# A fused attention and mixture kernel on one Trainium2 core: keys and queries loaded in whole rows, heads multiplied in 64-row tiles

## The chip, the cores and the metric

The kernel runs on one core of a Trainium2 chip. The metric is the device time of one execution in microseconds, and the time of a kernel is the median of its runs. TensorE (PE) multiplies; VectorE (DVE), ScalarE (ACT) and GpSimd (POOL) do the elementwise work; SyncE (SP) and POOL issue the transfers.

## The reference, cut to what matters

Two attentions with 32 packed queries per head, then a feed-forward layer, then a mixture of eight experts. Only the attention and what it hands on are touched by the change.

```python
def sm_attn(qq, kk, vv):                      # softmax(qq kk^T / sqrt(64)) vv
    ...
p_packed = sm_attn(p, k, v)                   # p: 4 x 8 x 32 x 64, k and v: 4 x 8 x 576 x 64
out = sm_attn(q, p_packed, p_packed)          # q: 4 x 8 x 576 x 64
x = out.transpose(0, 2, 1, 3).reshape(2304, 512)
h = x @ moe_w_in                              # 512 x 2048, in 64-bit floats
x = (h * clip(h + 3, 0, 6) / 6) @ moe_w_out   # 2048 x 512
...                                           # routing and eight experts, 512 x 1024 x 512 each
```

## The kernel before, in words

**An order written by a planner.** The kernel is a list of operations with costs, priorities, buffers and dependences. `Order.run` walks through it when the kernel is built, with a clock for each engine (PE, DVE, ACT, POOL, and SP for its transfers), and takes at each step the operation that can start first. The result is a fixed order of instructions on each engine. On the chip an engine doesn't skip an instruction that still waits, so what stands behind it waits too. `copy` (lines 439 to 447) lets the planner put an eviction on ACT or DVE. `dma` (line 436) gives each transfer on SP a cost from the KiB named to it.

**Attention in eight units.** `attention(u)` (from line 639) does unit u = 2b + j, four heads of batch b. Its keys lie as `kp[g]`: 96 partitions of 6 positions each, and for each position the two heads of a pair side by side. The queries lie as `qp`: two halves of 64 partitions with 9 positions each, also with the heads of a pair side by side. Each head is loaded by its own DMA on SP (lines 657 to 664 and 687 to 695), whose contiguous pieces on the SBUF side are one position of one head, 64 floats or 256 bytes. Values (line 698) come in one DMA with six positions of a head, 1536 bytes, in a piece. Unit 1 uses buffers that are free early; units 0 and 2 to 7 share one set of k, q and v buffers.

**The steps of a unit on PE.** Keys are transposed (L721) and evicted to `kT`, with the 2 x 64 features of a pair on the partitions. The packed queries, doubled side by side by a POOL copy (L706), are transposed (L738), and multiplied by `maskb` while they are evicted (L743), so that a matmul over 128 rows picks one head of the pair. First scores are four matmuls, 128 rows by 64 columns (L763). Then come maximum, exponential and sum (L773 to L801); query transposes (L811) and their evictions to `qT`; transposes of the exponentials (L831); products with the values (L847), each for both heads of a pair, so that half of the result belongs to the wrong head; scaling by the reciprocal and by `maskz`, which zeroes that half (L858); two transposes (L872) and two evictions to `ppT`; second scores over 128 rows (L904); and a second softmax whose result is the operand `a2` of the first layer.

**Packed weights.** `packed_weights` (line 994) multiplies the packed values with the first-layer weights. For the first units of work it is called with one weight block, takes one PSUM bank and does four matmuls of 128 rows by 64 columns (L1008). Later it is called with two blocks, takes two banks, and does 64-row by 32-column tiles (L1014). The results are evicted by ACT (L1031) and DVE (L1036). Layers 1 and 2 (L1074 to L1076, L1108 to L1110, L1127 to L1129) follow.

**Around it.** While attention runs, 64-bit weights are loaded in pieces of 512 KB. Sixteen of these are issued by POOL (L533) and taken apart by ACT (L506, L510), DVE (L513, L514, L517) and POOL (L501). Attention's units, this decoding and the first layers stand mixed in each engine's order.

Of the kernel before, what the change touches and what calls it, by code (L numbers as in the profile page):

```python
# [67 lines left out]
V_KIB = 840  # L68
# [103 lines left out]
def tile_kernel(  # L172
# [168 lines left out]
    maskb = [x.tile([128, 2, NP], F32, name=f"maskb{i}") for i, x in enumerate((const, att))]  # L341
    maskz = [x.tile([128, 2, 2, D], F32, name=f"maskz{i}") for i, x in enumerate((const, att))]
# [294 lines left out]
    ppTs = [hold("ppT", [128, 2, 64]) for _ in range(NU)]  # L637

    def attention(u, p_sb):
# [13 lines left out]
        kp = [tile_of(f"k{g}", [PR, R, 2, D]) for g in range(2)]  # L653
        v_sb = tile_of("v", [PR, 4, R, D])
        qp = tile_of("q", [128, RQ, 2, D])
        pd = tile_of("pd", [128, 2, D], 2)
        for h in range(4):
            dma(
                288,
                lambda h=h: nc.sync.dma_start(  # L660
                    kp[h // 2].t[:, :, h % 2, :], k[b, 4 * j + h].rearrange("(p r) d -> p r d", r=R)
                ),
                fills=[kp[h // 2]], **kw,
            )
# [22 lines left out]
        for h in range(4):  # L687
            dma(
                288,
                lambda h=h: nc.sync.dma_start(  # L690
                    qp.t[64 * (h // 2):64 * (h // 2) + 64, :, h % 2, :],
                    q[b, 4 * j + h].rearrange("(p r) d -> p r d", r=RQ),
                ),
                fills=[qp], **kw,
            )
# [18 lines left out]
        kT = tile_of("kT", [128, 2, S])  # L714
        for g in range(2):
            for a in range(2):
                ps = bank()

                def trans(g=g, a=a, ps=ps):
                    for r in range(3):  # L720
                        nc.tensor.transpose(  # L721
                            ps.t[:, r * PR:(r + 1) * PR],
                            kp[g].t[:, 3 * a + r].rearrange("p h d -> p (h d)"),
                            ident[:PR, :PR],
                        )

                pe(0.25, trans, reads=[kp[g]], writes=[ps], takes=[kT], **kw)
                copy(
                    lambda g=g, a=a: kT.t[:, g, a * HS:(a + 1) * HS],
                    lambda ps=ps: ps.t[:, :HS], HS, reads=[ps], fills=[kT], **kw,  # L730
                )


        ps = bank()
        pt = tile_of("pt", [128, 2, 2 * NP], 2)
# [5 lines left out]
        dve(  # L741
            t_dve(128),
            lambda ps=ps: nc.vector.tensor_tensor(  # L743
                pt.t,
                ps.t[:, :128].rearrange("p (g c) -> p g c", g=2),
                maskb[j].rearrange("p h n -> p (h n)")[:, None, :].to_broadcast([128, 2, 2 * NP]),
                ALU.mult,
            ),
            reads=[ps], writes=[pt], **kw,
        )  # L750

# [7 lines left out]
        for a in range(2):  # L759

            def scores(a=a):
                for g in range(2):
                    nc.tensor.matmul(  # L763
                        s1[a].t[64 * g:64 * g + 64, :HS],
                        pt.t[:, g, :],
                        kT.t[:, g, a * HS:(a + 1) * HS],
                        start=True, stop=True,
                    )
# [35 lines left out]
        qT = tile_of("qT", [128, 2, S])  # L804
        for r0 in range(0, RQ, 4):
            n = min(4, RQ - r0)
            ps = bank()

            def trans(r0=r0, n=n, ps=ps):
                for r in range(n):  # L810
                    nc.tensor.transpose(  # L811
                        ps.t[:, r * 128:(r + 1) * 128],
                        qp.t[:, r0 + r].rearrange("p h d -> p (h d)"),
                        ident,
                    )

            pe(0.11 * n, trans, reads=[qp], writes=[ps], takes=[qT], **kw)
            copy(
                lambda r0=r0, n=n: qT.t.rearrange("p g (r c) -> p g r c", c=64)[:, :, r0:r0 + n, :],
                lambda n=n, ps=ps: ps.t[:, :n * 128].rearrange("p (r g c) -> p g r c", g=2, c=64),  # L820
                n * 128, reads=[ps], fills=[qT], **kw,
            )
# [21 lines left out]
        def packed():  # L844
            for r in range(R):
                for g in range(2):
                    nc.tensor.matmul(  # L847
                        pp.t[64 * g:64 * g + 64, :128],
                        a1T.t[:, r, 64 * g:64 * g + 64],
                        v_sb.t[:, 2 * g:2 * g + 2, r, :],  # L850
                        start=(r == 0), stop=(r == R - 1),
                    )

        ppz = tile_of("ppz", [128, 2, 2 * D], 2)
        pe(1.55, packed, reads=[a1T, v_sb], writes=[pp], takes=[ppz], **kw)
        dve(
            t_dve(256),
            lambda: nc.vector.scalar_tensor_tensor(  # L858
                ppz.t,
                pp.t[:, None, :128].to_broadcast([128, 2, 128]),  # L860
                rc.t,
                maskz[j].rearrange("p g h d -> p g (h d)"),
                ALU.mult, ALU.mult,
            ),
# [4 lines left out]

        def trans(ps=ps):  # L870
            for g in range(2):
                nc.tensor.transpose(ps.t[:, 128 * g:128 * g + 128], ppz.t[:, g, :], ident)  # L872

        pe(0.22, trans, reads=[ppz], writes=[ps], takes=[ppT], **kw)

        for g in range(2):
            copy(
                lambda g=g: ppT.t[:, g, :],
                lambda g=g, ps=ps: ps.t[:, 128 * g + 64 * g:128 * g + 64 * g + 64],
                64, reads=[ps], fills=[ppT], **kw,  # L880
            )
# [4 lines left out]
        for tiles in (range(0, 6), range(6, RQ)):  # L886
# [10 lines left out]
            def scores(s2=s2, pairs=pairs, tail=tail):  # L897
                todo = [
                    (w, 128 * i + 64 * g, t + w, g) for i, t in enumerate(pairs) for g in range(2) for w in range(2)
                ]  # L900
                if tail:
                    todo += [(g, 128 * len(pairs), RQ - 1, g) for g in range(2)]
                for w, c, t, g in todo:
                    nc.tensor.matmul(  # L904
                        s2.t[64 * w:64 * w + 64, c:c + 64],
                        qT.t[:, g, 64 * t:64 * t + 64],
                        ppT.t[:, g, :],
                        start=True, stop=True,
                    )
# [84 lines left out]
    def packed_weights(i, b, w1s):  # L994
# [4 lines left out]
        tiled = len(w1s) > 1  # L999
        banks, got = [psum("ph") for _ in range(2 if tiled else 1)], [pair("pw", [128, 2, FG]) for _ in w1s]  # L1000

        def mm():
            for x, w1 in enumerate(w1s):
                for g in range(2):
                    for j in range(2):
                        pp = ppTs[2 * b + j].t[:, g, :]
                        if not tiled:
                            nc.tensor.matmul(  # L1008
                                banks[0].t[64 * g:64 * g + 64, j * FG:(j + 1) * FG], pp, w1.t[:, 2 * j + g, :],
                                start=True, stop=True,  # L1010
                            )
                        for h in range(2 * tiled):
                            r0, n0 = 64 * h, 32 * (h ^ j)
                            nc.tensor.matmul(  # L1014
                                banks[j].t[64 * g + n0:64 * g + n0 + 32, x * FG:(x + 1) * FG],
                                pp[r0:r0 + 64, n0:n0 + 32],
# [23 lines left out]
        for x, w in enumerate(got):  # L1040
            if not tiled:
                out_of(
                    banks[0], lambda: banks[0].t,
                    lambda i, w=w: w.t[i].rearrange("p j f -> p (j f)"), 2 * FG,
                )
            for j in range(2 * tiled):
# [721 lines left out]
    with tc.manual_schedule():  # L1768
# [3 lines left out]
        for j in range(2):  # L1772
            nc.vector.memset(maskb[j], 0.0)
            for h in range(2):
                nc.vector.memset(maskb[j][64 * h:64 * h + 64, h ^ j, :], 1.0)
            nc.vector.memset(maskz[j], 0.0)
            for g in range(2):
                for h in range(2):
                    r0 = 64 * g + 32 * h
                    nc.vector.memset(maskz[j][r0:r0 + 32, g, h ^ j, :], 1.0)  # L1780

# [201 lines left out]
```

## Time and profile before

| | us |
|---|---|
| median of 3 runs | 1895.11 |
| lowest and highest | 1893.11, 1896.27 |
| the profiled execution's own time | 1896.55 |
| its span, first to last instruction | 1894.8 |
| PE busy | 1860.7 (98%) |
| DVE, ACT, POOL busy | 1452.2, 884.4, 1202.6 |

The times are for all three layers; attention ends within the first 140 us. A share of busy time is an average over stages with different limits, so the first 107 us are read below in stretches of their own. In the rows, PE is the matmuls and PEld the weight loads, and a number in brackets with an arrow is the time that an engine sat idle before the instruction, and what ended it.

### The profile page before, as it was taken

The page shows a single profiled execution, that of the slowest core. Times are in us where ns is not written, and L with a number is a line of the kernel's source. Part 1 is how long each engine was busy: PE and PEld are TensorE (multiplying, and loading weights), DVE is VectorE, ACT ScalarE, POOL GpSimd, SP SyncE. Part 2 cuts the span into 40 slices and gives each one's busy share as a digit, 9 for nine tenths or more (in the row PEclk, how much of TensorE's full clock was granted, in tenths as well). Part 3 has the DMA queues.
Part 4 walks back from the last instruction along what each step waited for, and adds up shares of the span by engine and source line. Part 5 has one row for each costly group of instructions (what it writes and reads, how often), then busy time and mean ns, then how long its engine had stood idle before and what let it go on. Part 6 is the DMA issues. An engine that isn't in the chain of part 4 may idle for free.

```text
span 1894.8 us, 31056 instructions
## 1 busy us (share of the span) xinstructions
PE 1860.7 (98%) x11199; PEld 1772.8 (94%) x11199; DVE 1452.2 (77%) x2367; ACT 884.4 (47%) x1931; POOL 1202.6 (63%) x1101
## 2 busy tenths in 40 slices
PE   6999999999999999999999999999999999999998
PEld 4889999898989999999999999999999999999998
DVE  5877687666887777787777877878797787787877
ACT  5765664455556565556543333333334233333332
POOL 3536586665768786778664665656676566565664
PEclk9999999999999999999999999999999999999999
DMA  9844335633677777877787777777778777777773
GB/s 207 204 117 145 128 105 206 223 129 134 210 248 283 269 273 247 300 271 262 276 306 249 264 257 268 252 257 261 263 246 276 252 258 264 261 256 258 261 252 109
DMA packets 190874, 440.70 MB, mean 233 GB/s; under 512 B 51728, under 2 KB 98976, under 8 KB 178432
## 3 DMA queue, kind: packets, MB, share of 16 engines
q1 hardware_dynamic: 187760, 429.31, 67.4%
q0 software_dynamic: 2480, 8.62, 1.6%
q8 instruction: 88, 1.44, 0.3%
q10 hardware_dynamic: 480, 0.79, 0.1%
q14 instruction: 66, 0.54, 0.1%
HBM read 316.42 MB, written 122.23 MB: 232 GB/s over the span
## 4 chain that ended last, share of the span: by engine, by line
PE 86%; DVE 4%; DMA 3%; POOL 3%; ACT 2%; issue 1%; SPq 1%; DVEq 0%; POOLq 0%; ACTq 0%
PE ph L1261 12%; PE ph L1259 12%; PE ph L1260 12%; PE po L1505 8%; PE po L1506 8%; PE po L1504 8%; PE po L1612 5%; PE po L1614 5%; PE po L1613 5%; PE po L1127 1%; PE po L1128 1%; PE po L1129 1%; DMA rawE<-in_moe_w_dram 1%; PE ph L1074 1%; PE ph L1076 1%
## 5 line engine op out<-in xcount | busy, mean ns | idle before, releaser
L1459 POOL TENSOR_TENSOR tmp<-tmp,tmp 128x384 f32<-128x384 f32 x153 | 168.7, 1103 | 354.5 <-DVE tmp L1236 353.4
L579 POOL TENSOR_TENSOR hs<-tmp,hs 128x384 fp32r<-128x384 f32 x212 | 232.6, 1100 | 170.8 <-ACT hs L574 163.9
L1446 ACT ACTIVATE xy<-tmp 128x384 fp32r<-128x384 f32 x324 | 162.1, 521 | 323.8 <-DVE tmp L1236 285.6
L1453 POOL TENSOR_TENSOR xy<-tmp,xy 128x384 fp32r<-128x384 f32 x228 | 275.4, 1220 | 7.3 <-ACT xy L1446 5.0
L1516 DVE TENSOR_TENSOR acc<-po,acc 128x384 f32<-128x384 f32 x302 | 165.8, 550 | 99.3 <-PE po L1506 97.9
L1273 DVE TENSOR_TENSOR tmp<-ph,tmp 128x384 f32<-128x384 f32 x288 | 159.5, 554 | 86.2 <-PE ph L1261 84.6
L453 ACT ACTIVATE tmp<-ph 128x384 f32<-128x384 f32 x280 | 137.1, 490 | 172.7 <-PE ph L1261 169.0
L1504 PE MATMUL po<-xy,w2s 128*128 128x384 f32 x640 | 215.0, 336 | 1.3 <-ACT tmp L453 1.3
L1506 PE MATMUL po<-xy,w2s 128*128 128x384 f32 x640 | 215.6, 337 | 0.0
L1505 PE MATMUL po<-xy,w2s 128*128 128x384 f32 x640 | 215.5, 337 | 0.0
L1261 PE MATMUL ph<-ax,w 128*128 128x384 f32 x576 | 193.5, 336 | 0.0
L1259 PE MATMUL ph<-ax,w 128*128 128x384 f32 x576 | 193.4, 336 | 0.0
L1260 PE MATMUL ph<-ax,w 128*128 128x384 f32 x576 | 193.2, 335 | 0.0
L1636 DVE SCALAR_TENSOR_TENSOR acc<-po,Pr,acc 128x512 f32<-128x512 f32 x168 | 125.0, 745 | 73.8 <-PE po L1614 73.6
L1612 PE MATMUL po<-w,hs 128*128 128x512 f32 x384 | 151.4, 394 | 0.0
L1614 PE MATMUL po<-w,hs 128*128 128x512 f32 x384 | 150.8, 393 | 0.0
L1613 PE MATMUL po<-w,hs 128*128 128x512 f32 x384 | 149.9, 390 | 0.0
L1236 DVE SCALAR_TENSOR_TENSOR tmp<-tmp,PB 128x384 f32<-128x384 f32 x192 | 138.6, 722 | 5.3
L574 ACT ACTIVATE hs<-tmp 128x384 fp32r<-128x384 f32 x224 | 117.1, 524 | 51.0 <-DVE tmp L1088 46.2
L1446 ACT ACTIVATE ax<-tmp 128x384 fp32r<-128x384 f32 x124 | 62.8, 521 | 142.0 <-DVE tmp L1236 129.9
L1504 PEld LDWEIGHTS po<-xy,w2s 128*128 128x128 f32 x640 | 120.2, 188 | 1.7 <-ACT tmp L453 1.6
L1505 PEld LDWEIGHTS po<-xy,w2s 128*128 128x128 f32 x640 | 120.3, 188 | 0.0
(276 smaller groups left out, 5445.2 us busy)
## 6 DMA issues: line engine op xcount, KB each, us to landing
w2s<-w2d SPq DMA_DIRECT2D x224, 512.0 KB, 4.5
w<-w1d SPq DMA_DIRECT2D x64, 1024.0 KB, 6.0
w1x<-w1d SPq DMA_DIRECT2D x64, 768.0 KB, 5.7
raw<-in_moe_w_dram SPq DMA_DIRECT2D x64, 512.0 KB, 6.5
w1d<-w SPq DMA_DIRECT2D x32, 1024.0 KB, 5.0
w2d<-w SPq DMA_DIRECT2D x96, 256.0 KB, 2.5
w1d<-w1x SPq DMA_DIRECT2D x32, 768.0 KB, 5.6
rawE<-in_moe_w_dram SPq DMA_DIRECT2D x20, 512.0 KB, 4.6
```

Source lines behind the costliest of these rows:

```text
L579: lambda e: e.tensor_tensor(dst(w.t[1]), src(), as_f32(dst(w.t[0])), ALU.subtract),
L1259: nc.tensor.matmul(out, wh[:, at + c, :], bh[:, c, :], start=first and c == 0, **on)
L1260: nc.tensor.matmul(out, wh[:, at + c, :], bl[:, c, :], start=False, **on)
L1261: nc.tensor.matmul(out, wl[:, at + c, :], bh[:, c, :], start=False, **on)
L1446: A_SBUF, lambda: nc.scalar.activation(dst(0), t.t, AF.Copy),
L1453: lambda e: e.tensor_tensor(dst(1), t.t, as_f32(dst(0)), ALU.subtract),
L1504: nc.tensor.matmul(o, wh[:, f, cs], ah[:, f, :], start=begin and f == 0, **on)
L1505: nc.tensor.matmul(o, wh[:, f, cs], al[:, f, :], start=False, **on)
L1506: nc.tensor.matmul(o, wl[:, f, cs], ah[:, f, :], start=False, **on)
L1612: nc.tensor.matmul(ps.t, hh[:, f, ts], wh[:, f, :], start=(f == 0), stop=False)
L1613: nc.tensor.matmul(ps.t, hh[:, f, ts], wl[:, f, :], start=False, stop=False)
L1614: nc.tensor.matmul(ps.t, hl[:, f, ts], wh[:, f, :], start=False, stop=(f == NFC - 1))
```

## The change

Keys and queries are loaded two heads at a time, each partition taking its 6 or 9 positions of a head as one contiguous piece (1536 and 2304 bytes). On the partitions after the transpose stand two positions of one head, in place of one position of two heads. So a matmul works on 64 rows: the packed queries and values stand twice, once for each half, and no mask is needed. The masks and their memsets go, and a tile `spare` of 64 floats takes some of their room. Each part of the diff, cut to its core:

```diff
-        for h in range(4):
-            dma(288, lambda h=h: nc.sync.dma_start(
-                kp[h // 2].t[:, :, h % 2, :], k[b, 4 * j + h].rearrange("(p r) d -> p r d", r=R)), ...
+        for g in range(2):
+            dma(V_KIB / 2, lambda g=g: nc.sync.dma_start(
+                kp[g].t.rearrange("p h r d -> p h (r d)"),
+                k[b, 4 * j + 2 * g:4 * j + 2 * g + 2].rearrange("h (p r) d -> p h (r d)", r=R)), ...
@@ queries alike: two DMAs in place of four @@
-        dve(t_dve(128), lambda: tensor_tensor(pt.t, ps..., maskb[j]..., ALU.mult), ...)
+        copy(lambda: pt.t..., lambda ps=ps: ps.t[:, :128], 128, ...)
 first scores, for each of two banks a
-                for g in range(2):
-                    nc.tensor.matmul(s1[a].t[64 * g:64 * g + 64, :HS],
-                        pt.t[:, g, :], kT.t[:, g, a * HS:(a + 1) * HS], ...)
+                rows = slice(64 * a, 64 * a + 64)
+                for x in range(4):
+                    nc.tensor.matmul(s1[a].t[32 * x:32 * x + 32, :HS],
+                        pt.t[rows, x, :], kT.t[rows, x ^ j, :], ...)
 queries: 8 transposes of 128 x 128 as before and, for the ninth position, in place of one more:
+            for g in range(2):
+                for hh in range(2):
+                    nc.tensor.transpose(ps.t[:64 * g + 64, ...], qp.t[:, hh, RQ - 1 - g:]..., ident)
+        for g in range(2):
+            copy(lambda half=half: qT.t[half, RQ - 1]..., ..., 128, ...)
 products with the values, for each of six r
-                for g in range(2):
-                    nc.tensor.matmul(pp.t[64 * g:64 * g + 64, :128],
-                        a1T.t[:, r, 64 * g:64 * g + 64], v_sb.t[:, 2 * g:2 * g + 2, r, :], ...)
+                for x in range(4):
+                    nc.tensor.matmul(pp.t[32 * x:32 * x + 32, :D],
+                        a1T.t[:, r, 32 * x:32 * x + 32], v_sb.t[:, x ^ j, 2 * (r % 3) + r // 3, :], ...)
-        dve(t_dve(256), lambda: scalar_tensor_tensor(ppz.t, pp..., rc.t, maskz[j]..., ...))
+        dve(t_dve(128), lambda: tensor_scalar_mul(ppz.t, pp.t[:, None, :D].to_broadcast([128, 2, D]), rc.t), ...)
 ppT: one transpose and one copy of 128 x 128 in place of two transposes and two copies of 128 x 64
 second scores: 36 matmuls of 64 rows and 32 columns of ppT in place of 18 of 128 rows and 64 columns
-                        s2.t[64 * w:64 * w + 64, c:c + 64], qT.t[:, g, 64 * t:64 * t + 64], ppT.t[:, g, :],
+                        s2.t[r0:r0 + 64, c:c + 32], qT.t[r0:r0 + 64, r, at:at + 64], ppT.t[r0:r0 + 64, x, :],
@@ packed_weights: always the tiled form @@
-        banks, got = [psum("ph") for _ in range(2 if tiled else 1)], ...
+        banks, got = [psum("ph") for _ in range(2)], ...
+                                banks[j].t[32 * n0:32 * n0 + 32, x * FG:(x + 1) * FG],
+                                ppTs[2 * b + j].t[r0:r0 + 64, n0, :], w1.t[r0:r0 + 64, 2 * j + g, :], ...
```

V_KIB is 840. In second scores r0 is 0 or 64, for the rows and for the output's partitions alike. A call of `packed_weights` with one weight block does eight tiled matmuls in place of four, and evicts two results of 256 columns in place of one of 512.

## Rows read from the trace of the kernel before

**Rows 1.** The page's 40 slices of the span, 47.4 us each, in tenths busy.
```profile
PE   6999999999999999999999999999999999999998
DMA  9844335633677777877787777777778777777773
```
**Rows 2.** Busy time by stretch; columns: us, PE, PEld, DVE, ACT, POOL, PEclk, DMA share, GB/s.
```profile
30.00:40.00 10.00, 9.24 (x91) 7.08 (x91) 9.22 (x18) 6.03 (x15) 6.86 (x6) 0.66 1.14 199
100.00:107.00 7.00, 4.67 (x20) 4.45 (x21) 7.00 (x21) 5.12 (x13) 3.93 (x5) 0.77 0.30 94
0.00:52.00 52.00, 34.78 (x296) 25.01 (x297) 29.80 (x96) 28.33 (x70) 19.04 (x31) 0.91 1.09 203
52.00:107.00 55.00, 52.05 (x512) 44.43 (x512) 47.89 (x125) 42.38 (x110) 28.85 (x32) 0.97 0.83 195
```
**Rows 3.** Timeline of PE: start, us, line, and the idle time before it.
```profile
18.48 0.69 PE L721 MATMUL tp<-ident,unit_hs 96*128 96x96 f32 x6 [1.13 <-DMA unit_hs<-in_k_dram]
20.39 0.44 PE L721 MATMUL tp<-ident,unit_hs 96*128 96x96 f32 x3 [1.22 <-DMA unit_hs<-in_k_dram]
43.74 0.69 PE L721 MATMUL tp<-ident,k 96*128 96x96 f32 x6 [2.02 <-DMA k<-in_k_dram]
47.49 0.69 PE L721 MATMUL tp<-ident,k 96*128 96x96 f32 x6 [1.65 <-DMA k<-in_k_dram]
101.44 1.06 PE L811 MATMUL tp<-ident,q 128*128 128x128 f32 x8 [1.63 <-issue]
103.39 0.44 PE L1074 MATMUL ph<-ax,pwh 128*128 128x384 f32 x1 [0.89 <-DVE tmp L1088]
```
**Rows 4.** Timeline of the first 8 us: transfers on SP, and POOL's first copy.
```profile
0.74 2.75 SPq L660 DMA_DIRECT2D k<-in_k_dram  x4
...
7.73 0.28 POOL L706 COPY pd<-p 128x128 f32<-128x128 f32 x1 [2.93 <-DMA p<-in_p_dram]
```
**Rows 5.** DMA view of 20 to 33 us: packets, queues (packets, MB, share of 16 engines), keys' issues.
```profile
DMA packets 5735, 2.92 MB, mean 225 GB/s; under 512 B 5093, under 2 KB 5477, under 8 KB 5733
...
q1 hardware_dynamic: 5445, 1.85, 90.1%
q0 software_dynamic: 288, 1.05, 28.5%
...
k<-in_k_dram SPq DMA_DIRECT2D x4, 144.0 KB, 9.3
```
**Rows 6.** Two links of the chain that ended last, in order of time: start, us, what.
```profile
35.82 11.53 DMA k<-in_k_dram
...
90.02 8.48 DMA raw<-in_moe_w_in_dram
```
**Rows 7.** Timeline of PE: one call each of the products that the change touches.
```profile
67.21 1.14 PE L811 MATMUL tp<-ident,q 128*128 128x128 f32 x9
68.61 1.09 PE L1008 MATMUL ph<-w1f,ppT 128*64 128x256 f32 x8
72.22 1.53 PE L847 MATMUL tp<-v,a1T 96*64 96x128 f32 x24
77.08 1.27 PE L904 MATMUL tp<-ppT,qT 128*64 128x64 f32 x36
78.17 1.14 PE L763 MATMUL tp<-kT,pt 128*64 128x288 f32 x8
165.35 1.09 PE L1014 MATMUL ph<-w1f,ppT 64*32 64x256 f32 x32
```
**Rows 8.** Groups by line and shape, 0 to 135 us: count, busy us and mean ns, idle before.
```profile
L743 DVE TENSOR_TENSOR pt<-tp,maskb 128x128 f32<-128x128 f32 x8 | 2.3, 292 | 6.2 <-PE tp L738 6.2
L858 DVE SCALAR_TENSOR_TENSOR ppz<-tp,rc,maskz 128x256 f32<-128x256 f32 x8 | 3.8, 478 | 1.8 <-PE tp L847 1.8
L443 ACT ACTIVATE qT<-tp 128x128 f32<-128x128 f32 x6 | 1.7, 276 | 0.9 <-PE tp L811 0.9
L1031 ACT ACTIVATE pwh<-ph 128x512 fp32r<-128x512 f32 x6 | 3.6, 606 | 0.2 <-PE ph L1008 0.2
```

More of the change, by code (lines that the diff above doesn't have):

```diff
@@ L340, in tile_kernel @@
     ones = const.tile([128, 128], F32, name="ones")
-    maskb = [x.tile([128, 2, NP], F32, name=f"maskb{i}") for i, x in enumerate((const, att))]
-    maskz = [x.tile([128, 2, 2, D], F32, name=f"maskz{i}") for i, x in enumerate((const, att))]
+    const.tile([128, 64], F32, name="spare")
     biases = const.tile([128, 2], F32, name="biases")
@@ L635, in operand @@
         return pair("xy", [128, KC // 2, TB])
-    ppTs = [hold("ppT", [128, 2, 64]) for _ in range(NU)]
+    ppTs = [hold("ppT", [128, 4, NP]) for _ in range(NU)]
     def attention(u, p_sb):
@@ L686, in attention @@
         p_at = b if j else max(b - 1, 0)
-        for h in range(4):
+        for g in range(2):
             dma(
[L689 to L692, printed above, removed]
+                V_KIB / 2,
+                lambda g=g: nc.sync.dma_start(
+                    qp.t[64 * g:64 * g + 64].rearrange("p h r d -> p h (r d)"),
+                    q[b, 4 * j + 2 * g:4 * j + 2 * g + 2].rearrange("h (p r) d -> p h (r d)", r=RQ),
                 ),
@@ L711, in attention, with trans @@
         turns.setdefault("pd0", turns["pd"])
-        kT = tile_of("kT", [128, 2, S])
-        for g in range(2):
[L716 to L731, printed above, removed]
+        kT = tile_of("kT", [128, 4, HS])
+        for h in range(4):
+            ps = bank()
+            def trans(h=h, ps=ps):
+                for r in range(R // 2):
+                    nc.tensor.transpose(
+                        ps.t[:, r * PR:(r + 1) * PR],
+                        kp[h // 2].t[:, h % 2, 2 * r:2 * r + 2].rearrange("p r d -> p (r d)"),
+                        ident[:PR, :PR],
+                    )
+            pe(0.25, trans, reads=[kp[h // 2]], writes=[ps], takes=[kT], **kw)
+            copy(lambda h=h: kT.t[:, h], lambda ps=ps: ps.t[:, :HS], HS, reads=[ps], fills=[kT], **kw)
         ps = bank()
-        pt = tile_of("pt", [128, 2, 2 * NP], 2)
+        pt = tile_of("pt", [128, 4, NP], 2)
         pe(
@@ L740, in attention @@
         )
[L741 to L749, printed above, removed]
+        copy(
+            lambda: pt.t.rearrange("p x n -> p (x n)"), lambda ps=ps: ps.t[:, :128], 128, reads=[ps], writes=[pt], **kw
         )
@@ L801, in attention, with trans @@
         dve(0.08, lambda: nc.vector.reciprocal(rc.t, rc.t), writes=[rc], **kw)
-        qT = tile_of("qT", [128, 2, S])
-        for r0 in range(0, RQ, 4):
-            n = min(4, RQ - r0)
+        qT = tile_of("qT", [128, RQ, 128])
+        for hh in range(2):
             ps = bank()
-            def trans(r0=r0, n=n, ps=ps):
-                for r in range(n):
+            def trans(hh=hh, ps=ps):
+                for r in range(4):
                     nc.tensor.transpose(
                         ps.t[:, r * 128:(r + 1) * 128],
-                        qp.t[:, r0 + r].rearrange("p h d -> p (h d)"),
+                        qp.t[:, hh, 2 * r:2 * r + 2].rearrange("p r d -> p (r d)"),
                         ident,
                     )
-            pe(0.11 * n, trans, reads=[qp], writes=[ps], takes=[qT], **kw)
+            pe(0.44, trans, reads=[qp], writes=[ps], takes=[qT], **kw)
             copy(
-                lambda r0=r0, n=n: qT.t.rearrange("p g (r c) -> p g r c", c=64)[:, :, r0:r0 + n, :],
-                lambda n=n, ps=ps: ps.t[:, :n * 128].rearrange("p (r g c) -> p g r c", g=2, c=64),
-                n * 128, reads=[ps], fills=[qT], **kw,
+                lambda hh=hh: qT.t[:, 4 * hh:4 * hh + 4].rearrange("p r c -> p (r c)"), lambda ps=ps: ps.t,
+                512, reads=[ps], fills=[qT], **kw,
+            )
+        ps = bank()
+        def trans(ps=ps):
+            for g in range(2):
+                for hh in range(2):
+                    at = 256 * g + 128 * hh
+                    nc.tensor.transpose(
+                        ps.t[:64 * g + 64, at:at + 128], qp.t[:, hh, RQ - 1 - g:].rearrange("p r d -> p (r d)"), ident
+                    )
+        pe(0.44, trans, reads=[qp], writes=[ps], takes=[qT], **kw)
+        for g in range(2):
+            half = slice(64 * g, 64 * g + 64)
+            copy(
+                lambda half=half: qT.t[half, RQ - 1].rearrange("p (h c) -> p h c", h=2),
+                lambda half=half, ps=ps, g=g: ps.t[half, 256 * g:256 * g + 256].rearrange(
+                    "p (h c) -> p h c", h=2
+                )[:, :, 64 * g:64 * g + 64],
+                128, reads=[ps], fills=[qT], **kw,
             )
@@ L845, in packed @@
             for r in range(R):
-                for g in range(2):
+                for x in range(4):
                     nc.tensor.matmul(
-                        pp.t[64 * g:64 * g + 64, :128],
-                        a1T.t[:, r, 64 * g:64 * g + 64],
-                        v_sb.t[:, 2 * g:2 * g + 2, r, :],
+                        pp.t[32 * x:32 * x + 32, :D],
+                        a1T.t[:, r, 32 * x:32 * x + 32],
+                        v_sb.t[:, x ^ j, 2 * (r % 3) + r // 3, :],
                         start=(r == 0), stop=(r == R - 1),
                     )
-        ppz = tile_of("ppz", [128, 2, 2 * D], 2)
-        pe(1.55, packed, reads=[a1T, v_sb], writes=[pp], takes=[ppz], **kw)
-        dve(
[L857 to L864, printed above, removed]
+        ppz = tile_of("ppz", [128, 2, D], 2)
+        pe(1.0, packed, reads=[a1T, v_sb], writes=[pp], takes=[ppz], **kw)
+        dve(
+            t_dve(128),
+            lambda: nc.vector.tensor_scalar_mul(ppz.t, pp.t[:, None, :D].to_broadcast([128, 2, D]), rc.t),
             reads=[pp, rc], writes=[ppz], **kw,
@@ L868, in attention @@
         ppT = ppTs[u]
[L870 to L881, printed above, removed]
+        pe(
+            0.12,
+            lambda ps=ps: nc.tensor.transpose(ps.t[:, :128], ppz.t.rearrange("p a d -> p (a d)"), ident),
+            reads=[ppz], writes=[ps], takes=[ppT], **kw,
+        )
+        copy(
+            lambda: ppT.t.rearrange("p x n -> p (x n)"), lambda ps=ps: ps.t[:, :128], 128, reads=[ps], writes=[ppT], **kw
+        )
         w = a2[b]
@@ L998, in packed_weights @@
         kw, quick = prios(i)
-        tiled = len(w1s) > 1
-        banks, got = [psum("ph") for _ in range(2 if tiled else 1)], [pair("pw", [128, 2, FG]) for _ in w1s]
+        banks, got = [psum("ph") for _ in range(2)], [pair("pw", [128, 2, FG]) for _ in w1s]
         def mm():
@@ L1005, in mm @@
                     for j in range(2):
-                        pp = ppTs[2 * b + j].t[:, g, :]
-                        if not tiled:
+                        for h in range(2):
+                            r0, n0 = 64 * h, 2 * g + (h ^ j)
                             nc.tensor.matmul(
[L1009 to L1016, printed above, removed]
+                                banks[j].t[32 * n0:32 * n0 + 32, x * FG:(x + 1) * FG],
+                                ppTs[2 * b + j].t[r0:r0 + 64, n0, :],
                                 w1.t[r0:r0 + 64, 2 * j + g, :],
@@ L1040, in packed_weights @@
         for x, w in enumerate(got):
[L1041 to L1046, printed above, removed]
+            for j in range(2):
                 out_of(
@@ L1771, in tile_kernel @@
         nc.vector.memset(two_, 2.0)
[L1772 to L1780, printed above, removed]
         place("p0", att, 1)
```

31 lines of the change are left out of this document (16 added, 15 removed).

## The prediction

> **What bounds the kernel now.** I read the page's slices first [rows 1]. PE is 90% busy or more in almost every slice; the first, at 6 tenths, is the exception, and there the DMA engines stand at 9. The table by stretch sharpens this [rows 2]: from 0 to 52 us PE is busy for 34.78 of 52 us, DVE for 29.80, ACT for 28.33, and only the DMA engines are full (a share of 1.09; packets overlap, so it can pass 1). From 52 to 107 us PE has 52.05 of 55 us and DVE 47.89: here they bound the time together. After that PE hardly stops, so a microsecond that PE gains early moves all that follows, and the end. The question is which waits keep PE idle early. The timeline names them [rows 3]: keys of unit 1 (1.13 and 1.22 us), keys of unit 3 (2.02 and 1.65), and at 101 to 103 us 1.63 and 0.89. The chain of waits says the same with the whole flights [rows 6]: keys of unit 3 were 11.53 us under way, a piece of weights 8.48 us.
>
> **Why the flights are long.** From 20 to 33 us, about one unit, 5093 of 5735 packets are under 512 B [rows 5]; these are the 256-byte pieces of keys and queries. Thirteen us of 16 engines are 208. SP's queue took 90.1% of it, 187; POOL's took 28.5%, 59, for 1.05 MB in 288 packets, which is 17.8 KB per us. Values (0.59 MB, long packets) at that rate are 33, so that 154 are left for 5093 small packets: 30 ns each. Keys and queries of a unit are 8 x 144 KB = 1.18 MB; in long packets at 17.8 KB per us they would take 66. The stretch's 246 would be 158, and 13 us would be **8.4 us** where the DMA engines are the limit. Of the 642 packets of 512 B and more, 288 are POOL's; the other 354 are about as many as the 384 pieces of the values, so whole rows of 1536 bytes do become long packets.
>
> **The change part by part.** Numbers are microseconds, against the profiled execution.
>
> First unit. Four key issues take 2.75 [rows 4]; two fewer let the packed queries leave 1.4 sooner, and POOL's first copy waits for just them (2.93). I take -1.4.
>
> Keys of unit 1. By the ratio 8.4/13 their data come early enough for both waits to go: -2.35 [rows 3].
>
> Keys of unit 3. 11.53 [rows 6] becomes 7.4, which is 4.1 less, more than the two waits of together 3.67 [rows 3]: -3.7. What is late next is the softmax chain on DVE and ACT, which in 43 us instead of 52 would be 69% and 66% busy, so it fits.
>
> Clock. From 30 to 40 us the granted clock is 0.66 of 2.4 GHz on average [rows 2], so about two thirds of it at the lower level, 1.2 GHz, after a stretch with idle gaps. That costs 0.34 x 9.24 = 3.1. Nothing to all of it may come back; I take half, -1.6, since some gaps stay.
>
> Weights at 90 to 103 us. The 8.48 [rows 6] at the same ratio would be 5.5; behind it lie 2.52 of idle PE [rows 3] and 0.23 x 4.67 = 1.1 of lower clock [rows 2]. DVE is full in that stretch (7.00 of 7.00), so I take half: -1.8, between 0 and -3.6.
>
> PE, per unit [rows 7]. The tiled L1014 does 32 matmuls of 256 columns in 1.09, 34 ns each; the untiled L1008 does 8 of the same length in 1.09, 136 ns each. So 64 x 32 tiles run four times as many at once. First scores: 8 in 1.14 become 16, at four times the rate 0.57, -0.57 (bounds 0 and -0.57). Second scores: 36 in 1.27, 35 ns each, become 72 with half the columns. Bounds are no cost, if short ones run side by side, and +1.27; since no row, at 64 columns or 256, comes below 34 ns, I take +1.27. Products with the values: 24 in 1.53 become 48; half of the columns would give -0.76, 34 ns each +0.10; I take +0.10 by the same row. Queries: 12 transposes for 9 in 1.14, +0.38; packed values: one fewer, -0.13. Together +1.05. Of eight units, six (2 to 7) run their second scores after 52 us, where PE counts: +6.3. In units 0 and 1 PE's idle time hides it; without that cover it is 2.1 more.
>
> Packed weights. Eight calls of L1008 become tiled: half as long by the row above, 8 x 0.55 = -4.4; nothing, if two banks have to be emptied first.
>
> DVE and ACT [rows 8]. DVE loses 0.29 (mask of `pt`) and about 0.19 (L858 at 128 columns, priced as L743) in each unit, 3.8 in all; ACT gains `pt` and a second tail of the queries, 0.28 each, and loses up to 0.28 at `ppT`. Each packed call evicts two of 256 for one of 512: between 0.276 and 0.606 that is 0.39 twice, +0.17 on each engine, 1.4 for eight. So DVE -2.4, ACT up to +6. ACT idles 12.6 of 52 to 107 us [rows 2], which hides it: 0; were ACT the bound, up to +6. The mask memsets lie in DVE's idle start: 0, and no more than 2 gained.
>
> Queues. No wait is added on SP; it issues four transfers fewer per unit. POOL keeps its order: 0.
>
> Sum: -1.4 - 2.35 - 3.7 - 1.6 - 1.8 + 6.3 - 4.4 = -9.0. The profiled execution took 1896.55, 1.4 above the median of 1895.11; its sum gives 1887.6, and against the median 1886.1. I predict 1886.
>
> The second scores are where a rule speaks against the change. The row is 35 ns for a matmul of 64 columns [rows 7]. The Trainium skill, "TensorEngine Tiling (Array Packing)", Performance Considerations, says that a matmul carries an overhead of about 60 cycles, so that one column costs as much as 60, and that no tiling should be taken out of a dimension already small. By that figure 72 would take an estimated 1.8 us, and the sum would be -13.4 instead of -9.0; the row decides.
>
> **The rivals.**
>
> The engines are the bound behind the DMA. Only unit 3's waits go, since the chain of unit 0 to 2 runs through ACT and DVE in the planner's order, and PE's own +1.9 stays: 1893. For it: DVE 47.89 of 55 after 52 us. Against: 57% before [rows 2].
>
> Tiled matmuls do not overlap, and it becomes slower. Second scores now run two halves of 64 columns at 35 ns each. If the two row halves exclude each other, a matmul stands alone at 70 ns, and 72 take 5.0: +3.8 per unit, 22.6 in six in place of 7.6 by my term. The sum is then +6: 1901. It decides from where a call takes 2.54 + 9.0 / 6 = 4.0, at which the gain is used up. Against it: L1014 has both row halves in one bank and yet 34 ns [rows 7]. The Trainium skill's same page, Restrictions and Gotchas, says that different row tiles cannot access one PSUM bank at once; the second scores put both row halves in one bank. L1014's row contradicts that for its shape.
>
> More than the waits comes back. All of PE's 17.2 idle of the first 52 us but some 5, an estimate for the landing of the first keys (their issues alone end at 3.5 [rows 4]), both clock losses and the late gap, with the PE terms at zero: 12.2 + 3.1 + 3.6 = 18.9, so 1876. Against it: the softmax chain leaves gaps of its own.
>
> Long rows stay short packets, so that only issues get fewer: about 1895. The values' packets [rows 5] speak against it.
>
> **How the numbers follow.** A measurement of this kernel can tell about 0.2%, 3.8 us, from no change. My forecast, 1880 to 1891, has 0.61; the larger gain 0.13; the engines as bound and the short packets together 0.15, which counts as no change; slower 0.11. Faster is then 0.74, the same 0.15, slower 0.11. The range 1876 to 1894 takes in the forecast, the larger gain, and most of the no-change cases; it leaves out the slower one and the ends, about 2 in 10.
>
> **What would show it.** Right: few packets under 512 B in the first 50 us; flights of keys near 7 us; PE's steady stretch starting near 43 us instead of 52; a L904 call of about 2.5 us; packed calls near 0.55. Wrong: PE waiting in the first 52 us for DVE or ACT as long as it did for keys, second scores of 4 us and more, or PE idle at packed calls for a bank.

## The result, and the profile after

The changed kernel is slower: 1904.49 us (median of 4 runs, 1901.9 to 1905.76) against 1895.3 for the kernel before beside it; the ratio is 1.0054, with an interval of 1.0039 to 1.0069 (the two medians alone give 1.0048). The profiled execution took 1904.52, 7.97 more than that of before. The page after, its slices of 47.6 us each:

```profile
PE   7998999999999999999999999999999999999998
...
DMA  8743325643577777777787777777778777777773
```

Against [rows 1] the DMA engines are a tenth lower in several of the first six slices, and PE's first slice rises from 6 to 7 tenths. But the fourth slice of PE, full before, is now at 8; it holds the answer. By stretch, with the columns of [rows 2]:

```profile
30.00:40.00 10.00, 8.54 (x108) 6.13 (x109) 7.36 (x17) 5.41 (x16) 3.89 (x5) 0.52 0.71 200
60.00:70.00 10.00, 8.89 (x75) 8.61 (x76) 5.27 (x18) 5.76 (x15) 2.18 (x2) 0.66 0.46 110
0.00:52.00 52.00, 41.88 (x583) 31.64 (x584) 29.17 (x84) 33.42 (x89) 20.70 (x34) 0.90 0.89 224
52.00:107.00 55.00, 52.11 (x827) 44.56 (x826) 43.25 (x125) 43.11 (x115) 20.57 (x21) 0.94 0.71 185
141.00:157.00 16.00, 9.94 (x58) 7.42 (x56) 9.32 (x15) 7.96 (x18) 7.78 (x7) 0.68 0.53 186
```

In the first 52 us PE works 7.1 us more than before and DMA's share falls from 1.09 to 0.89, as forecast; the clock from 30 to 40 us fell further, from 0.66 to 0.52. Another low stretch, 0.66 from 60 to 70 us, is new. So is the last row, and it matters most: in 16 us from 141 on PE is busy for 9.94, at a clock of 0.68. Before, it was busy for all of that stretch:

```profile
141.00:157.00 16.00, 16.00 (x111) 15.05 (x110) 12.18 (x16) 9.94 (x20) 10.14 (x8) 1.00 0.55 191
```

**Where it stands at a common point.** Both kernels reach a point at which PE has done the same work in attention and in layers 1 and 2, and turns to the next packed weights. Timelines of PE there (start, us, line), the changed kernel first:

```profile
141.29 0.34 PE L1061 MATMUL ph<-ax,pwl 128*128 128x384 f32 x1
146.15 2.96 PE L1004 MATMUL ph<-w1f,ppT 64*32 64x256 f32 x32 [4.51 <-DVE pwl L1026]
150.65 0.69 PE L1059 MATMUL ph<-ax,pwh 128*128 128x384 f32 x1 [1.54 <-DVE pwl L1026]
...
154.65 0.52 PE L1112 MATMUL po<-hs,w 128*128 128x384 f32 x1
```

And the kernel before:

```profile
142.97 0.34 PE L1076 MATMUL ph<-ax,pwl 128*128 128x384 f32 x1
143.24 2.00 PE L1008 MATMUL ph<-w1f,ppT 128*64 128x256 f32 x16
145.17 0.45 PE L1074 MATMUL ph<-ax,pwh 128*128 128x384 f32 x1
...
147.37 0.34 PE L1127 MATMUL po<-hs,w 128*128 128x384 f32 x1
```

At the first of these rows the changed kernel is 1.68 us ahead (141.29 against 142.97). At the last, with two packed calls (x32 here, x16 there) and four triples of layer 1 between, it is 7.28 behind (154.65 against 147.37). The stretch between the two rows takes 13.36 us in place of 4.40, and this swing of 8.96 us is more than the whole difference of 7.97. PE waits 4.51 and 1.54 for `pwl`, the DVE instruction that empties the packed weights' banks, and works at a lower clock behind it (0.68 on average, by the last row of the table by stretch): neighbouring layer-1 products start 0.32 us apart instead of 0.17.

**Why `pwl` is late.** The timeline of DVE in the changed kernel shows it idle for 8.27 us, and `pwl` behind that gap:

```profile
135.46 0.28 DVE L513 TENSOR_SCALAR ms<-ms 128x256 uint32<-128x256 uint32 x1
144.01 0.69 DVE L1341 TENSOR_TENSOR TE<-rawE 128x512 f32<-128x512 f32 x1 [8.27 <-DMA wg<-in_moe_w_gate_dram]
145.67 0.76 DVE L1026 TENSOR_TENSOR pwl<-ph,pwh 128x256 fp32r<-128x256 f32 x2 [0.97 <-ACT pwh L1021]
```

`TE` takes apart a piece `rawE` of the experts' 64-bit weights, for a later layer. It stands ahead of `pwl` in DVE's fixed order, and ACT's `HE` (L1347), made from `TE`, stands ahead of `pwh` (L1021) in ACT's; its idle time of 3.77 us there ends on `TE`. The row names `wg` as what ended DVE's wait, but `TE` reads `rawE` alone, and the chain of waits names that, in a link of 6.99 us:

```profile
136.63 6.99 DMA rawE<-in_moe_w_dram
144.01 0.70 DVE TE L1341
144.73 0.63 ACT HE L1347
```

SP's queue shows why it left no earlier. It issues three raw pieces in an entry of 17.07 us, the last of which must wait for DVE's `ms` to free a buffer at 135.5:

```profile
118.91 17.07 SPq L532 DMA_DIRECT2D raw<-in_moe_w_in_dram  x3
136.63 0.37 SPq L532 DMA_DIRECT2D rawE<-in_moe_w_dram  x1
```

In the kernel before, the same piece left at 139.28, behind attention's last PE instruction (138.87), and the first `TE` ran at 144.50 without a wait of DVE.

**What else answers to the rows of before.** DMA view from 20 to 33 us, as in [rows 5]:

```profile
DMA packets 1843, 3.49 MB, mean 269 GB/s; under 512 B 143, under 2 KB 1329, under 8 KB 1841
...
k<-in_k_dram SPq DMA_DIRECT2D x2, 288.0 KB, 8.5
```

PE's waits from 0 to 160 us in the changed kernel (line, releaser, us in total, times, longest):

```profile
PE tp L721 <- DMA k<-in_k_dram: 4.7, 2, 4.2
PE ph L1004 <- DVE pwl L1026: 4.5, 1, 4.5
PE ph L1059 <- DVE pwl L1026: 1.5, 1, 1.5
PE tp L901 <- issue: 1.4, 1, 1.4
```

And before:

```profile
PE tp L721 <- DMA k<-in_k_dram: 9.6, 4, 5.3
PE tp L721 <- DMA unit_hs<-in_k_dram: 2.3, 2, 1.2
```

Small packets fall from 5093 to 143, and PE's waits for keys from 11.9 to 4.7, nearly all of it the first landing of 4.2. The flights of keys in that window shrank less than forecast, from 9.3 us [rows 5] to 8.5, where near 7 was to be a sign of being right. The products, in rows that answer to [rows 7]; first scores both with their two banks one behind the other (x16) and apart (x8). The trace counts each matmul of the program twice here (transposes once), so that the 36 second scores of a unit are 72:

```profile
70.95 0.88 PE L852 MATMUL tp<-v,a1T 96*32 96x64 f32 x48
73.83 0.71 PE L752 MATMUL tp<-kT,pt 64*32 64x288 f32 x16
74.47 2.31 PE L901 MATMUL tp<-ppT,qT 64*64 64x32 f32 x72
76.71 0.66 PE L1004 MATMUL ph<-w1f,ppT 64*32 64x256 f32 x16
77.31 1.10 PE L797 MATMUL tp<-ident,q 128*128 128x128 f32 x8
78.24 0.60 PE L814 MATMUL tp<-ident,q 128*64 128x128 f32 x4
...
85.94 0.71 PE L752 MATMUL tp<-kT,pt 64*32 64x288 f32 x8
...
88.81 0.69 PE L752 MATMUL tp<-kT,pt 64*32 64x288 f32 x8
```

### The profile page after: what moved, and what is told of

It reads as the page before. It is cut to its first block, busy times and chain, and to the rows that moved or that the text cites. A ratio compares the mean times of both kernels' runs of the same rounds, so it can differ in the third digit from the quotient of the medians.

```text
span 1902.7 us, 32254 instructions
## 1 busy us (share of the span) xinstructions
PE 1870.0 (98%) x11823; PEld 1779.1 (94%) x11823; DVE 1445.5 (76%) x2351; ACT 888.0 (47%) x1949; POOL 1204.3 (63%) x1099
## 4 chain that ended last, share of the span: by engine, by line
PE 85%; DVE 5%; DMA 3%; POOL 3%; ACT 2%; issue 1%; SPq 0%; DVEq 0%; POOLq 0%; ACTq 0%
PE ph L1244 12%; PE ph L1246 12%; PE ph L1245 12%; PE po L1491 8%; PE po L1490 8%; PE po L1489 8%; PE po L1597 5%; PE po L1599 5%; PE po L1598 5%; DMA rawE<-in_moe_w_dram 1%; PE po L1112 1%; PE po L1114 1%; PE po L1113 1%; PE tp L901 1%; PE ph L1059 1%
```

## The experiments

The theory: the loads and products do about what they should, and a reordering of DVE and ACT, by which `TE` stands ahead of the packed weights' evictions and waits for a late transfer, costs about 9 us. The rivals: the 72 second scores cost it; the packed weights' second bank costs it; whole rows bring less than assumed. Each run's ratio is to the kernel before, on the same chip; where two edited kernels are compared, the difference of their ratios is taken, times 1895 us. By the intervals such a difference is good to 3 to 5 us, and a ratio can differ from the quotient of two medians by up to 0.1%. In the new kernels line numbers differ by up to two.

**`TE` planned later, in the changed kernel (a1_late).** A transfer was planned to land 2 us after its issue; the first two `rawE` are planned with 12, and nothing else is edited. In the trace PE's order is the same as in the changed kernel; DVE's and ACT's differ from 141 us on.

```diff
-        return order.op([("SP", max(0.6, kib / 350.0), fn)], lat=2.0, **kw)
+        kw.setdefault("lat", 2.0)
+        return order.op([("SP", max(0.6, kib / 350.0), fn)], **kw)
...
-                raws = [second_raw(G1 + 2 * d2 + n, 101, "rawE", turns["l1"]) for n in range(2)]
+                raws = [second_raw(G1 + 2 * d2 + n, 101, "rawE", turns["l1"], 12.0 if i == 1 else 2.0) for n in range(2)]
```

> The changed kernel, with one number of the planner altered: the first two loads of second-layer weights (rawE) are planned to land 10 us later than before, so that the planner puts the DVE and ACT instructions which need them (TE, HE) behind the evictions of the packed weights, not ahead of them. Theory of the stall: between 141.6 and 156.6 us of the changed kernel DVE and ACT wait at the head of their queues for rawE (issued at 136.63, landed about 143.6), so the packed weights' banks stay full, PE idles 4.5 + 1.5 us and then runs at the lower clock; without it 7 to 9 us come back: about 1896. Rival, the instructions: the loss is PE's own added work in the second scores, and the stall only shows where it would have waited anyway: within 2 us of 1904.

Measured: 1895.72, ratio 1.0004 (0.9991 to 1.0017). The issue of `rawE` hardly moves, at 136.72, but `TE` now stands behind six `pwl` at 147.75, and the packed calls run almost at once. Its timeline of PE:

```profile
142.05 2.07 PE L1005 MATMUL ph<-w1f,ppT 64*32 64x256 f32 x32 [0.32 <-DVE pwl L1027]
144.28 0.44 PE L1060 MATMUL ph<-ax,pwh 128*128 128x384 f32 x1 [0.16 <-DVE pwl L1027]
...
146.47 0.34 PE L1113 MATMUL po<-hs,w 128*128 128x384 f32 x1
```

And of DVE:

```profile
141.57 0.75 DVE L1027 TENSOR_TENSOR pwl<-ph,pwh 128x256 fp32r<-128x256 f32 x2 [5.75 <-ACT pwh L1022]
...
147.75 1.54 DVE L1342 TENSOR_TENSOR TE<-rawE 128x512 f32<-128x512 f32 x1
```

From the common point (141.39 here) to the layer-2 row it now takes 5.08 us, not 13.36. So the stall was the loss: taken out, 0.50% or 9.5 us come back (1.0054 to 1.0004). The second scores and the banks are still there, so neither by itself is the 9 us. But nothing is won over the kernel before, either.

**The same edit in the kernel before (b1_late_before).** A control: does the planner's number help without the stall?

> A control: the kernel before with the same altered number as a1_late (the first two rawE loads planned to land 10 us later). The stall theory says that the kernel before has no such stall, since rawE is issued there at 139.28 us, lands about 144.4, and PE is still at work till 145: no change, within 2 us of the kernel before. If the altered plan is better in itself, whatever the stall: 5 to 9 us faster, as it was on the changed kernel.

Measured: 1894.61, ratio 0.9996 (0.9986 to 1.0006). No change, though `TE` moves behind `pwl` here too. The edit is worth 9 us only where `TE` stood in the way.

This run's trace shows something more. All its orders are those of the kernel before up to 142 us, so for attention it is a second execution of that kernel. PE's waits for keys are 7.1 us in it, not 11.9:

```profile
PE tp L722 <- DMA k<-in_k_dram: 5.9, 2, 5.2
PE tp L722 <- DMA unit_hs<-in_k_dram: 1.2, 1, 1.2
```

In its timeline of PE unit 3's two key transposes, which stood behind 2.02 and 1.65 us of waiting in [rows 3], no longer wait for keys, and the common point comes at 140.32 instead of 142.97:

```profile
42.83 0.71 PE L722 MATMUL tp<-ident,k 96*128 96x96 f32 x6 [0.15 <-ACT qT L444]
45.80 0.86 PE L722 MATMUL tp<-ident,k 96*128 96x96 f32 x6 [0.18 <-DVE ax L978]
...
140.32 0.34 PE L1077 MATMUL ph<-ax,pwl 128*128 128x384 f32 x1
```

In the traces of a3_scores32 and b2_tiles_before, which load as the kernel before does, unit 3's keys aren't waited for either. So two executions differ by 2.65 us at the common point, and the changed kernel's 141.29 lies between them. The stretch behind it takes 4.40 us in both, so the swing of 8.96 isn't touched by this.

**Second scores in halves, in the kernel before (a3_scores32).** Each matmul of a call (36 in the trace) is cut into two of 32 columns; rows, masks, loads and order stay.

```diff
-                    nc.tensor.matmul(s2.t[64 * w:64 * w + 64, c:c + 64], ..., ppT.t[:, g, :], ...)
+                    for n0 in (0, 32):
+                        nc.tensor.matmul(s2.t[64 * w:64 * w + 64, c + n0:c + n0 + 32], ..., ppT.t[:, g, n0:n0 + 32], ...)
```

> The kernel before with one part of the change's cost alone: each second-score matmul of 64 columns is cut into two of 32, still on 128 rows and with the masks, so that 36 instructions on PE become 72 in a unit, each with its own weight load of 64 columns; order and all else the same. The instruction theory: about 1.0 us in each of eight units, all on the path: +8, 1903. If units 0 and 1 hide theirs in idle PE time: +5 to +6, 1901. If short matmuls run beside each other: no change.

Measured: 1900.87, ratio 1.0033 (1.0021 to 1.0044), which is 6.3 us of 1895. The call took the same time as the changed kernel's, on 128 rows instead of 64:

```profile
77.72 2.31 PE L905 MATMUL tp<-ppT,qT 128*64 128x32 f32 x72
```

Twice as many instructions with half the columns cost 2.31 for 1.27, and with an unchanged order that comes through to the end: six units' worth is 6.2 us, as in the case that units 0 and 1 hide theirs. It is a real cost of the change, near the predicted one.

**Packed weights always tiled, in the kernel before (a4_banks).**

```diff
-        tiled = len(w1s) > 1
+        tiled = True
```

> The kernel before with the packed weights always in the tiled form (two banks, eight matmuls of 64 x 32, two evictions of 256 columns) for the first units too; the rest as before, the order as the planner then makes it. If only PE's time counts: 8 x 0.43 = 3.4 us faster, 1892. If two banks of the few that there are cost waits: 2 to 6 us slower, with PE idle at L1014 or at L1074 for DVE's pwl.

Measured: 1899.18, ratio 1.0021 (1.0011 to 1.0031). The slowdown, 4.0 us, lies in the range expected of waits for banks, but it isn't made of them: PE waits 0.5 us for `pwl`. What grew is another wait, by its waits from 0 to 160 us:

```profile
PE tp L721 <- DMA k<-in_k_dram: 17.0, 6, 4.9
...
PE ph L1014 <- DVE pwl L1036: 0.5, 1, 0.5
```

The planner gave a new order, in which keys are late six times. The gain of the shorter calls, forecast at 4.4 (3.4 in the expectation), seems to be lost in that; the edit alone, with the old order, wasn't tried.

**First scores and values in tiles, in the kernel before (b2_tiles_before).** First scores on 64 rows by 32 columns, values on 32 columns for one head; masks, loads and second scores stay.

```diff
-                    nc.tensor.matmul(s1[a].t[64 * g:64 * g + 64, :HS], pt.t[:, g, :], kT.t[:, g, a * HS:(a + 1) * HS], ...)
+                    for h in range(2):
+                        r0, n0 = 64 * h, 32 * (h ^ j)
+                        nc.tensor.matmul(s1[a].t[64 * g + n0:64 * g + n0 + 32, :HS],
+                            pt.t[r0:r0 + 64, g, n0:n0 + 32], kT.t[r0:r0 + 64, g, a * HS:(a + 1) * HS], ...)
@@ values alike: four matmuls of a1T.t[:, r, 32 * x:32 * x + 32] in place of two @@
```

> The kernel before with two parts of the change alone that cost PE less in the changed kernel's trace: first scores in 64 x 32 tiles (0.65 in place of 1.12 us a unit) and products with the values in 96 x 32 tiles (0.81 in place of 1.46), on its own data, masks and order. If every unit's PE time counts: 8 x 1.12 = 9 us faster, 1886. If units 0 to 2 wait for keys anyway: 5 to 6 us faster, 1889. If PE then waits at the next late thing (keys, rawE): 0 to 2 us.

Measured: 1895.55, ratio 1.0001 (0.9991 to 1.001), no gain. Its timeline of PE says first which calls shrank:

```profile
69.03 0.88 PE L849 MATMUL tp<-v,a1T 96*32 96x64 f32 x48
...
74.82 1.17 PE L765 MATMUL tp<-kT,pt 64*32 64x288 f32 x16
```

The values did, 0.88 for 1.53. The first scores did not, 1.17 for 1.14, where the changed kernel's take 0.71: here the two row halves write into one bank, there each half has its own (banks `s1[a]`, rows of half `a`). So this run tests the values alone, some 0.65 x 6 = 3.9 us after 52 us. By the interval no more than 1.7 us of it came to the end. The waits of PE from 52 to 107 us suggest where the rest went: 2.0 us, in single pieces of up to 0.8, for `ax` (DVE), `ppT` (ACT) and `ppz` (DVE), none of which the kernel before has in that stretch. Two single traces can't prove that, since two executions of one order differ by more (b1_late_before). DVE stays as busy as before there:

```profile
52.00:107.00 55.00, 50.58 (x583) 42.46 (x582) 48.17 (x122) 43.10 (x112) 30.12 (x31) 0.97 0.81 190
```

So of a microsecond less on PE less than half came off the end here, though one more was about one more (a3_scores32).

**Small pieces again, in the changed kernel (a2_pieces).** Keys and queries in 256-byte pieces, in 16 DMAs a unit; the order stays that of the changed kernel.

```diff
-        for g in range(2):
-            dma(V_KIB / 2, lambda g=g: nc.sync.dma_start(
-                kp[g].t.rearrange("p h r d -> p h (r d)"), ...
+        for h in range(4):
+            dma(V_KIB / 4, lambda h=h: [nc.sync.dma_start(
+                kp[h // 2].t[:, h % 2, t::2], k[b, 4 * j + h].rearrange("(p r) d -> p r d", r=R)[:, t::2]) for t in range(2)], ...
```

> The changed kernel with its keys and queries loaded in pieces of 256 bytes again (each head in two DMAs that take every other position), all compute and the planned order the same. If the whole rows gave what the wait rows of before suggest, this is 5 to 9 us slower than the changed kernel (1910 to 1913), with about 5000 packets under 512 B per unit again and PE waiting some 6 to 10 us more for keys in the first 52 us. The stall theory says it is less, 2 to 5 us, because PE comes later to the place where it waits for rawE anyway. If the loads were hidden all along: within 2 us of 1904.

Measured: 1922.39, ratio 1.014 (1.0121 to 1.0158), 0.86% or 16.3 us above the changed kernel, more than any of the three cases allowed. PE waits 22.6 us for keys in ten places. But the edit changes two things, pieces and the number of transfers, so it was taken apart.

**The same number of transfers, long pieces (b3_split16).** 16 DMAs a unit with contiguous pieces of 768 to 1280 bytes: `t` above becomes `slice(0, 3)` and `slice(3, 6)`, for queries `slice(0, 5)` and `slice(5, 9)`.

> The changed kernel with as many key and query transfers as a2_pieces (16 in a unit), of the same bytes, but in pieces of 576 to 1280 bytes that are contiguous: 3 positions of a key row, 5 and 4 of a query row. If a2_pieces was slow for the size of its pieces: within 3 us of the changed kernel, 1904. If it was slow for the number of transfers: near 1920.

Measured: 1915.04, ratio 1.0104 (1.0086 to 1.0122), 0.50% or 9.5 us above the changed kernel. That is between what size and number alone would give, and nearer to number. SP's timeline of the first 16 us:

```profile
0.74 3.69 SPq L659 DMA_DIRECT2D k<-in_k_dram  x8
4.48 0.43 SPq L673 DMA_DIRECT2D p<-in_p_dram  x1
4.95 5.02 SPq L690 DMA_DIRECT2D q<-in_q_dram  x8
...
10.72 5.38 SPq L659 DMA_DIRECT2D unit_hs<-in_k_dram  x7
```

In the changed kernel two key issues take 0.89 and SP turns to unit 1 at 4.24; here it does so at 10.72, in a2_pieces at 12.85. Of the 16.3 us, 9.5 came with the number of transfers (and pieces shorter than the changed kernel's 1536 and 2304 bytes), and 6.8 with 256-byte pieces; each of the two is good to some 5 us. In the kernel before, with 8 transfers of keys and queries a unit, the share of each wasn't measured.

**Costs in the planner as measured (b4_late_true).** The edit of a1_late and, in the planner, the costs of PE's calls as the trace has them (the last is 0.25 less).

```diff
-            pe(0.55, scores, reads=[pt, kT]
+            pe(0.33, scores, reads=[pt, kT]
-        pe(1.0, packed, reads=[a1T, v_sb]
+        pe(0.82, packed, reads=[a1T, v_sb]
-            pe(0.15 * len(tiles), scores, reads=[qT, ppT]
+            pe(0.25 * len(tiles), scores, reads=[qT, ppT]
-                0.45 * len(w1s) + 0.4, mm,
+                0.45 * len(w1s) + 0.15, mm,
```

> a1_late with the planner's PE costs set to what the changed kernel's trace shows (first scores 0.33 a bank, values 0.82, second scores 0.25 a tile, packed weights 0.15 less); what is computed is the same. If wrong costs make the planner's order worse: 2 to 5 us faster than a1_late, 1891 to 1894. If the order is bound by what PE has to do: within 2 us of a1_late.

Measured: 1892.71, ratio 0.9985 (0.9974 to 0.9997): 0.69% or 13 us under the changed kernel, and 0.15% under the one before, the only version whose interval stays below 1. Against a1_late it is 0.19% or 3.6 us, in the range expected if wrong costs spoil the order, but just clear of noise; and the gain over the kernel before is under the 0.2% that I had set as what a measurement can tell.

## Why the prediction was wrong

By its own steps, 1886 was forecast and 1904.5 measured, outside the range and with the other sign.

**First unit: right. Keys: right in this trace, by luck.** The copy that waits for the packed queries starts at 6.19 instead of 7.73, 1.5 earlier (1.4 predicted). PE's waits for keys fell by 7.2 (7.4 predicted, with the first unit). But the term "Keys of unit 3 ... -3.7" was read from waits of one execution. In three further traces with the old loads (b1_late_before, a3_scores32, b2_tiles_before) PE doesn't wait for unit 3's keys at all, so in three of the four executions there was nothing to win. Against b1_late_before the waits for keys fell by 2.4, from 7.1 to 4.7. The 1.63 us of idle PE at 101 us, part of the term for the weights, isn't in that second execution either.

**PE's products: right for the largest, wrong for others.** Second scores +1.04 a call (2.31 for 1.27; +1.27 predicted; the run with halves alone confirms at the end that they cost). Packed weights -0.43 a call (-0.55). Queries take 1.53, from 77.31 to 78.84, for 1.14: +0.39 (+0.38). Values were forecast at +0.10, from 34 ns for any matmul; they took 0.88 for 1.53, -0.65, 18 ns each: that floor was read from products with other tiles and did not hold. First scores (-0.57 predicted) gave -0.43 where sixteen run at 0.71, in two of the eight units; in four units the calls stand apart or are interrupted, and twice 0.69 or more is no less than 1.14. On the whole the products were no dearer than forecast.

**The clock: wrong.** I let half of a loss of 3.1 come back. Reckoned in the same way, with PE's busy time from 0 to 52 and from 52 to 107 us, the low clock took an estimated 0.09 x 34.78 + 0.03 x 52.05 = 4.7 us before and 0.10 x 41.88 + 0.06 x 52.11 = 7.3 after: 2.6 more (1.5 more if one adds up stretches of 10 us). The waits are shorter, but the stretch from 30 to 40 us, now at 0.52, still stands behind idle time, and new low rows came at 60 to 70 us behind a gap of 1.38. Why the chip stays low that long was not tested.

**That PE's time is the end's time: half wrong.** I wrote that a microsecond that PE gains early moves all that follows. b2_tiles_before shows that a saving after 52 us need not. At the common point, where the eviction order plays no part yet, the sum of the steps was a gain of 7.9 us (without two of the eight packed calls, 1.1). The changed kernel stands there 1.68 us ahead of one execution of the kernel before and 0.97 behind the other, so about nothing was won, as the ratio of 1.0004 without the stall says too. Against the first execution 6.2 us are missing, and the clock accounts for an estimated 3.6 to 4.7 of them: 2.1 that were to come back (the 1.6 and half of 1.1), and 1.5 to 2.6 that were lost instead. Against the second 8.9 are missing, among them unit 3's 3.7. The rest I can't divide.

**The step that failed: "Queues. No wait is added on SP ... POOL keeps its order: 0."** I counted transfers on SP and looked at POOL, and did not ask what the planner would do with DVE's and ACT's order when attention ends earlier: at 128.1 (L963) instead of 139.1. The planner reckons with a landing of 2 us for the `rawE` transfers, and the chip does not keep that: 4.2 us in the kernel before, 7.2 in the changed one, by the DMA views from 134 to 146 us. `TE` came to stand ahead of the packed weights' evictions, and the next packed calls need those banks. 8.96 us of swing in the trace, 9.5 back in a1_late, nothing in b1_late_before: this cause of the loss is shown. That the planner moved `TE` because attention ends earlier is my reading; no run tests it alone. This step turned no change into a loss. That there was no gain in the first place lies in the terms above, unit 3's keys and the clock foremost.

Of the rivals, "it becomes slower" came true in sign and near in time (1901), but by luck and not by its mechanism: a second-score call takes 2.31, not 4.0 or more. Whether its row halves run side by side stays open, since on 128 rows, where there are no halves, 72 matmuls take 2.31 too (a3_scores32). "The engines are the bound behind the DMA" is nearest to what is left without the stall, 1895.7 for a forecast of 1893, but luck has a part in that too: the one gain it kept was unit 3's waits.

## What to carry to other kernels

Where a planner fixes each engine's order from estimated costs, a change of one part is a change of every queue: before counting a gain, ask which instruction will stand first on each engine, what transfer it waits for, and whether someone else's buffer hangs behind it. A load that nobody needs soon should be planned with the landing that the trace shows, or be consumed late. And a saving on the busiest engine may not count in a stretch where another engine is nearly as busy (here 52 and 48 of 55 us). Before a wait goes into a sum, look for it in the trace of a second execution: 3.7 us of this forecast stood in one trace of four.

## What the runs showed of the hardware that was not expected

**Short tiled matmuls.** 48 matmuls of 96 rows by 32 columns with 64 moving columns took 0.88 or 0.81 us, 17 to 18 ns each. With 64 columns in the stationary operand it was 32 ns (72 in 2.31), on 64 rows and on 128 alike, and 35 ns with twice the moving columns (36 in 1.27). So between these shapes it is not the moving columns that set this time. It could be the load of the stationary operand, or the number of column tiles that fit side by side: with four tiles of 32 columns, 4 x 17.5 = 70 ns for each, with two of 64 columns 2 x 32 = 64. Neither was tested by itself. The Trainium skill, "TensorEngine Tiling (Array Packing)", Performance Considerations, gives an overhead of about 60 cycles for a matmul, an estimated 25 ns at 2.4 GHz. The rows of 17 and 18 ns, with four column tiles in turn, lie below it.

**Row halves and banks.** Eight first-score matmuls of one row half into one bank take 0.69 us; sixteen, the other half into the other bank right behind, 0.71. With both halves in one bank, and the halves in turn, sixteen take 1.17. By the Trainium skill, "TensorEngine Tiling (Array Packing)", Restrictions and Gotchas, different row tiles cannot access one PSUM bank at once. The prediction weighed that against L1014's 34 ns and thought it contradicted. The rows of the first scores agree with the Trainium skill there. L1014 changes between two banks after every pair of halves, so that its row was no clean counterexample.

**The number of transfers.** Eight key transfers occupied SP for 3.69 us, and for 5.31 in 256-byte pieces; the changed kernel's two take 0.89.
